# One decode layer on one core: K and V in eight 4 MB transfers instead of sixteen of 2 MB, and the weights in fewer, wider pieces

## The chip, the cores and the metric

The kernel runs on one core of a Trainium2 chip. The metric is the device time of one execution in microseconds (us). A core has five engines that run side by side: TensorE (PE; its weight loads are shown as PEld), VectorE (DVE), ScalarE (ACT), GpSimd (POOL) and SyncE (SP). Sixteen DMA engines move data between the chip's memory and the core's SBUF. SP and ACT issue the transfers, each on a queue of its own (q1 for SP and q10 for ACT in the profile), and each transfer is spread over the DMA engines.

## What is computed

Two sequences (B = 2) with one new token each go through a layer whose attention and MLP both read the same normalised input and are summed. Only the last 2048 of 8192 cached positions count.

```python
xn = layernorm(x)                                   # [2, 1, 576]
q = (xn @ wq).reshape(2, 1, 32, 128)                # 32 query heads, 16 K/V heads, each used by 2
scores = q @ k_cache[:, :, 6144:8192].T * 128**-0.5
o = softmax(scores) @ v_cache[:, :, 6144:8192]
h = relu(xn @ w1 + b1) ** 2                         # 4608 wide
return x + o.reshape(2, 1, 4096) @ wo + (h @ w2 + b2)
```

Everything is bfloat16. K and V are 16.8 MB each after the cut, wq and wo 4.7 MB each, w1 and w2 5.3 MB each: 53.6 MB are read once for an output of 2.3 KB.

## The kernel before

**Units.** A unit `u` is one sequence and four of the 16 K/V heads (`TH = 4`, line 44), so there are eight units (`NU`, line 49). The K of a unit is one 2 MB transfer into a tile of 128 partitions with 16 KB each, and so is its V (`issue_kv`, line 121). Each partition gets 64 consecutive cached rows of one head, which lie together in memory. The pool `kvpool` (line 95) has six such tiles. A tile is refilled only when the tile that stood in it has been read: SP waits for that before it issues the next transfer, and whatever stands behind it on SP waits too.

**One unit's work** is `step(u)` (line 501). TensorE transposes K in eight groups of four 128x128 float32 blocks (`transposes`, line 313; a float32 holds two bfloat16), and ACT and DVE take turns to copy a group from PSUM to SBUF (lines 325 and 327). Three PSUM buffers (`kT`) hold the groups. `scores` (line 329) multiplies the transposed K by the queries, which are laid out with zeros so that one product of 32 columns serves several heads; `softmax` (line 344) takes the maximum (DVE line 346, POOL line 350), the exponential (ACT line 357) and transposes the result (DVE line 360). `pv` (line 364) multiplies V of the unit two before, and `pv_end` (line 376) picks the right head out of each product.

**Weights.** wq and w1 come as 512 full rows, four to a partition, and a remainder of 64 rows cut into two halves of columns (`issue_w`, line 129). wo comes in two halves (`issue_wo`, line 154). w2 comes in four blocks, the last one in three pieces (`issue_w2`, line 162, `W2P`, line 493), so that little work is left after the last piece. What doesn't fit into these blocks, 256 rows, is loaded by ACT in small transfers (`issue_w2x`, line 179): four of five partitions with 9216 bytes, and one of 96 partitions with 1152 bytes. `out_acc` (line 266) adds up all products with wo and w2 in PSUM, four matmuls of 144 columns for each row.

**Order.** TensorE's order is the program's (`keep_in_program_order`, line 105). The transfers of SP are issued in this order: K0, wq in two parts, K1, V0, K2, V1, K3, V2, K4, V3, K5, V4, K6, V5, K7, wo's first half, w1 in two parts, V6, V7, wo's second half, and six pieces of w2. Eight semaphores are handed out in turn to the transfers of both queues, so a transfer also waits until the one eight places before it has landed. After the last piece of w2 come four matmuls, a copy (line 573) and the store of the result (line 574).

Of the kernel before, what the change touches and what calls it, by code (L numbers as in the profile page):

```python
# [16 lines left out]
def kernel(  # L17
# [26 lines left out]
    TH = 4  # L44
# [3 lines left out]
    NQ = Hkv // TH  # L48
    NU = NQ * B
    JG = 8  # L50
    NG = NJ // JG
    UE = NJ * Dh
    NT = 2
    NS = 2 * NT
    NJJ = NJ // NS
    SR = NS * NC
    assert SR == 32 and NG % NT == 0

    NFULL = D // P
    REM = D - NFULL * P  # L60
    S = P // REM
    KC = NFULL + 1
    NXN = NFULL + S
    LQ = (Hq * Dh) // S
    L1 = F // S
    NG4 = 4
    QW = Hq * Dh // NG4
    QB = QW // 2
    QH = QW // Dh
    HW = F // NG4  # L70
    HB = HW // 3
    FR = HW // P
    XS = ((8, 20, 5), (1, 96, 96))
    FT = (HW - sum(r * p for r, p, _ in XS)) // P
    F3 = (NG4 - 1) * HW
    CX = [(r, FT, P) for r in range(FT)]
    FX = []
    for xr, xp, _ in XS:
        FX.append(F3 + FT * P + sum(m * n for m, n, _ in XS[:len(FX)]))
        CX += [(FX[-1] - F3 + r, xr, xp) for r in range(xr)]  # L80
    assert FX[-1] + XS[-1][0] * XS[-1][1] == F
    N3 = (NG4 - 1) * FR
    NFC = N3 + len(CX)
    RB = 32 * (NG4 - 1) + B
# [4 lines left out]
    NP = NQ // 2  # L89
    WR = 2 * NC * Dh // P  # L90
    assert Dh // WR == NC
# [3 lines left out]
    kvpool = ctx.enter_context(tc.tile_pool(name="kvpool", bufs=6))  # L95
    ktpool = ctx.enter_context(tc.tile_pool(name="ktpool", bufs=2))
    wbig = ctx.enter_context(tc.tile_pool(name="wbig", bufs=1))
    wrem = ctx.enter_context(tc.tile_pool(name="wrem", bufs=1))
    wopool = ctx.enter_context(tc.tile_pool(name="wopool", bufs=1))
# [9 lines left out]

    x2d = A_x.rearrange("b s d -> (b s) d")  # L110
    out2d = out.rearrange("b s d -> (b s) d")

    k_tiles, v_tiles, wq_tiles, w1_tiles, wo_tiles, w2_tiles = {}, {}, {}, {}, {}, {}
    WBW = max(Hq * Dh, F)
    WRW = max(LQ, L1)

    def unit_view(cache, u):
        tq, b = divmod(u, B)
        return cache[b, tq * TH:(tq + 1) * TH, S0:Sk, :].rearrange("h (c j) d -> c h (j d)", c=CP)

    def issue_kv(tiles, cache, u, name, parts=1):
        tl = kvpool.tile([P, UE], BF16, tag="kv", name=f"{name}_{u}")
        v = unit_view(cache, u)
        n = UE // parts
        tiles[u] = tl
        return [lambda i=i: nc.sync.dma_start(out=tl[:, i * n:(i + 1) * n], in_=v[:, :, i * n:(i + 1) * n])
# [478 lines left out]
```

## Time and profile before

| what | us |
|---|---|
| median of 3 runs (range) | 134.43 (134.38 to 134.54) |
| the profiled execution | 134.47 |
| its span, first to last instruction | 132.6 |
| PE busy / DVE busy / ACT busy | 84.1 / 57.2 / 46.7 |
| first packet of K0 moves, from the span's start | 2.18 |
| last piece of w2 has landed | 129.43 |
| output's copy ends | 130.08 |

The profiled execution took 134.47 us, 1.9 us more than its span: that much lies outside the first and last instruction. The store and the end of the program take from 130.08 to 132.6. A row of the profile that is cut into slices gives tenths: 9 is a busy share of 90% or more. The DMA row is a mean over the sixteen DMA engines. A chain of waits is followed back from the last instruction: each piece is the time in which the work named was what the next piece waited for.

### The profile page before, as it was taken

To read this page: it belongs to the slowest core of one execution; us is meant where nothing else is said; L and a number is where in the kernel's file an instruction comes from. 1 tells how busy PE (TensorE), PEld (TensorE's weight loads), DVE (VectorE), ACT (ScalarE), POOL (GpSimd) and SP (SyncE) were. 2 spreads that over 40 slices of the span, in tenths; PEclk is the share of its full clock that TensorE was granted. 3 is DMA by queue.
4 is the path that set the end of the run, shared out by engine and by line. 5 is a ranking of instruction groups with operands and counts; after the bars stand their busy time and mean duration, and the time that the engine had idled before them with its cause. 6 is when DMAs were issued, how large, how long until landed. Compare 5 with 4: busy or idle time off the path is not lost.

```text
span 132.6 us, 2337 instructions
## 1 busy us (share of the span) xinstructions
PE 84.1 (63%) x982; PEld 52.2 (39%) x982; DVE 57.2 (43%) x156; ACT 46.7 (35%) x64; POOL 5.2 (4%) x17
## 2 busy tenths in 40 slices
PE   0069409599597669298496599697500938655941
PEld 0068303257364436164254346354300424414930
DVE  6724400525477456566377446575400043344000
ACT  5715500418874375176265255194200040000000
POOL 6000000010010010100100100100100000000000
PEclk9999955958999999999999769999985595555595
DMA  4999999999999999999999999999999999999960
GB/s 139 409 415 488 425 397 416 430 430 415 444 418 431 433 420 427 431 430 430 418 440 420 440 430 432 421 457 432 478 405 388 425 425 450 407 423 428 416 247 1
DMA packets 4219, 53.76 MB, mean 405 GB/s; under 512 B 503, under 2 KB 730, under 8 KB 1246
## 3 DMA queue, kind: packets, MB, share of 16 engines
q1 hardware_dynamic: 4032, 53.32, 94.6%
q10 hardware_dynamic: 178, 0.31, 0.6%
q8 instruction: 7, 0.11, 0.3%
q14 instruction: 2, 0.02, 0.0%
HBM read 53.62 MB, written 0.00 MB: 404 GB/s over the span
## 4 chain that ended last, share of the span: by engine, by line
DMA 62%; PE 4%; DVE 1%; ACT 1%; issue 1%; ACTq 0%
DMA v<-in_A_v_cache_dram 29%; DMA w<-in_B_w_dram 17%; DMA k<-in_A_k_cache_dram 16%; PE kT_ps L108 3%; PE o_ps L105 1%; ACT kT L325 1%; PE sc_ps L105 1%; ACT p L357 1%; DVE pT L360 1%; DVE kT L327 0%; DVE o L386 0%; PE out_ps L105 0%; ACT fin_sb L573 0%; DVE o L384 0%; PE op_ps L105 0%
## 5 line engine op out<-in xcount | busy, mean ns | idle before, releaser
L108 PE MATMUL kT_ps<-ident_f,k 128*128 128x128 f32 x256 | 40.0, 303 | 9.3 <-DMA k<-in_A_k_cache_dram 7.0
L108 PEld LDWEIGHTS kT_ps<-ident_f,k 128*128 128x128 f32 x256 | 31.5, 155 | 22.6 <-issue 11.6
L325 ACT COPY kT<-kT_ps 128x1024 bf16<-128x1024 bf16 x32 | 32.0, 1012 | 21.8 <-PE kT_ps L108 17.4
L327 DVE COPY kT<-kT_ps 128x1024 bf16<-128x1024 bf16 x32 | 21.8, 682 | 12.9 <-PE kT_ps L108 12.7
L105 PE MATMUL sc_ps<-kT,qz 128*32 128x512 bf16 x128 | 10.3, 403 | 6.4 <-DVE kT L327 5.0
L357 ACT ACTIVATE p<-sc_ps,bias 128x512 bf16<-128x512 f32 x8 | 5.5, 688 | 17.6 <-DVE gown L353 17.6
L105 PE MATMUL o_ps<-v,pT 128*32 128x512 bf16 x128 | 11.6, 461 | 0.0
L105 PEld LDWEIGHTS <-xnT 128*2 128x2 bf16 x100 | 3.1, 112 | 17.7 <-issue 17.5
L105 PE MATMUL h_ps<-w_big,xnT 128*2 128x384 bf16 x48 | 3.6, 484 | 7.9 <-DMA w_big<-in_B_w_dram 7.9
L346 DVE TENSOR_REDUCE m<-sc_ps 128x1 f32<-128x512 f32 x8 | 5.5, 692 | 7.1 <-PE sc_ps L105 7.1
L386 DVE SCALAR_TENSOR_TENSOR o<-o_ps,in_s,o 128x128 f32<-128x128 f32 x24 | 8.3, 348 | 0.5
L360 DVE STREAM_TRANSPOSE pT<-p 128x512 bf16<-128x512 bf16 x8 | 5.7, 711 | 6.5 <-ACT p L357 6.5
L573 ACT CAST fin_sb<-out_ps 113x144 bf16<-113x144 f32 x1 | 0.3, 279 | 21.8 <-PE out_ps L105 21.8
L105 PE MATMUL q_ps<-wq_big,xnT 128*2 128x512 bf16 x32 | 3.6, 625 | 5.0 <-DMA wq_big<-in_A_wq_dram 5.0
L350 POOL PARTITION_ALL_REDUCE gmax<-m x8 | 2.9, 365 | 88.8 <-DVE m L348 88.8
L384 DVE TENSOR_SCALAR o<-o_ps,in_s 128x128 f32<-128x128 f32 x8 | 2.7, 341 | 8.1 <-PE o_ps L105 8.1
L451 DVE TENSOR_TENSOR hrow<-t 98x384 bf16<-98x384 f32 x3 | 1.6, 557 | 10.6 <-ACT t L450 10.5
L105 PEld LDWEIGHTS <-qz 128*32 128x32 bf16 x128 | 2.2, 96 | 10.1 <-DVE kT L327 7.5
L105 PE MATMUL op_ps<-o,of_h 128*128 128x129 f32 x16 | 3.9, 333 | 3.2 <-DVE o L386 3.2
L105 PEld LDWEIGHTS <-hT_sb 128*17 128x17 bf16 (+2 forms) x172 | 4.3, 116 | 3.2 <-issue 3.2
L105 PE MATMUL out_ps<-w,hT_sb 128*17 128x144 bf16 x136 | 4.1, 279 | 2.1 <-DMA w<-in_B_w_dram 2.0
L450 ACT ACTIVATE t<-h_ps 98x384 f32<-98x384 f32 x3 | 1.4, 489 | 11.0 <-PE h_ps L105 10.7
(74 smaller groups left out, 52.8 us busy)
## 6 DMA issues: line engine op xcount, KB each, us to landing
k<-in_A_k_cache_dram SPq DMA_DIRECT2D x8, 2048.0 KB, 18.3
v<-in_A_v_cache_dram SPq DMA_DIRECT2D x8, 2048.0 KB, 9.9
wo<-in_A_wo_dram SPq DMA_DIRECT2D x2, 2304.0 KB, 27.2
w_big<-in_B_w_dram SPq DMA_DIRECT2D x1, 4608.0 KB
wq_big<-in_A_wq_dram SPq DMA_DIRECT2D x1, 4096.0 KB, 17.8
w<-in_B_w_dram SPq DMA_DIRECT2D x3, 1296.0 KB, 31.6
w_rem<-in_B_w_dram SPq DMA_DIRECT2D x1, 576.0 KB, 28.0
w<-in_B_w_dram SPq DMA_DIRECT2D x1, 576.0 KB, 22.1
```

Of the source, the lines that this page charges most:

```text
L105: tc.keep_in_program_order(nc.tensor.matmul(*a, **k))
L108: tc.keep_in_program_order(nc.tensor.transpose(*a, **k))
L325: nc.scalar.copy(out=kT, in_=kT_ps[:])
L327: nc.vector.tensor_copy(out=kT, in_=kT_ps[:])
L346: nc.vector.tensor_reduce(out=m1[:], in_=sc_ps[:], axis=AX.X, op=ALU.max)
L350: nc.gpsimd.partition_all_reduce(gmax[:], m2[:], channels=P, reduce_op=ReduceOp.max)
L357: nc.scalar.activation(out=p_sb[:], in_=sc_ps[:], func=ACT.Exp, bias=bias[:, 0:1], scale=scale, accum_out=o1[:, Dh:Dh + 1])
L360: nc.vector.transpose(out=pT[:].rearrange("p j r -> p (j r)"), in_=p_sb[:])
L384: nc.vector.tensor_scalar(scalar1=in_s[:, 0:1], scalar2=None, op0=ALU.mult, **kw)
L386: nc.vector.scalar_tensor_tensor(scalar=in_s[:, k:k + 1], in1=o1[:, 0:Dh], op0=ALU.mult, op1=ALU.add, **kw)
L450: nc.scalar.activation(out=t1, in_=mlp["ps"][k][0:RB, :], func=ACT.Relu)
L451: nc.vector.tensor_tensor(out=hrow[:, k * HB:(k + 1) * HB], in0=t1, in1=t1, op=ALU.mult)
```

## The change

The units become twice as large and half as many: eight K/V heads of one sequence (`TH = 8`), 128 consecutive rows or 32 KB in each partition, four units. A K or V is one 4 MB transfer, `kvpool` holds three of them, and there are sixteen groups of transposes in a step. The scores of a unit are now four banks wide and are computed in four chunks, each followed by its own maximum on DVE; the exponential and the transpose of the result are one instruction each over 2048 columns instead of 512 (and four of each instead of eight). There is one score buffer instead of two. `pv(u)` follows a step of a later unit as a whole: 64 matmuls of 256 columns instead of 16 of 512 for a unit half as large.

wq and w1 are read flat: 4.5 rows in each partition, one transfer each, and the normalised input is laid out with zeros so that each half row meets its own input. wo is one transfer into the same tile that held wq and w1. w2 is two halves of 18 rows in each partition: the first is one transfer, the second has four pieces of 9, 5, 2 and 1 rows, and the last row of each partition comes on ACT's queue in three parts (85, 32 and 11 partitions).

SP has 16 transfers instead of 28, in this order: K0, wq, K1, V0, K2, V1, w1, K3, V2, V3, wo, w2's first half, and four pieces of its second half. The small transfers on ACT's queue are all issued before the first copy of transposed K; before, they were spread over the first 55 us. TensorE's order follows that of the transfers. The waits of SP that come from tiles: K2 for the transposes of K0, V1 for those of K1, K3 for `pv(0)`, V2 for the transposes of K2, V3 for `pv(1)`, wo for the products with w1, w2's halves for the transposes of K3 and for `pv(2)`.

```diff
-    TH = 4
+    TH = 8
...
-    NT = 2
-    NS = 2 * NT
+    NS = 2
...
+    W2P = [(0, 9), (9, 14), (14, 16), (16, 17)]
+    XS = [(0, 85), (85, 117), (117, 128)]
...
-    kvpool = ctx.enter_context(tc.tile_pool(name="kvpool", bufs=6))
-    ktpool = ctx.enter_context(tc.tile_pool(name="ktpool", bufs=2))
+    kvpool = ctx.enter_context(tc.tile_pool(name="kvpool", bufs=3))
     wbig = ctx.enter_context(tc.tile_pool(name="wbig", bufs=1))
-    wrem = ctx.enter_context(tc.tile_pool(name="wrem", bufs=1))
-    wopool = ctx.enter_context(tc.tile_pool(name="wopool", bufs=1))
+    ktpool = ctx.enter_context(tc.tile_pool(name="ktpool", bufs=4))
...
+    def issue_flat(w, name):
+        n = w.shape[0] * w.shape[1] // P
+        tl = wbig.tile([P, NH * L1], BF16, tag="wbig", name=name)
+        nc.sync.dma_start(out=tl[:, 0:n], in_=w.rearrange("r n -> (r n)").rearrange("(p l) -> p l", p=P))
+        return tl
...
+    k_tiles[0] = issue_kv(A_k_cache, 0, "k")
+    wq_sb = issue_flat(A_wq, "wq")
+    k_tiles[1] = issue_kv(A_k_cache, 1, "k")
+    v_tiles[0] = issue_kv(A_v_cache, 0, "v")
...
+    def scores(u, n):
...
+        matmul(sc, lhsT=far_h[:], rhs=is_h, start=True, stop=False, skip_group_check=True)
+        kT = kT_tiles.pop((u, n))[:].rearrange("p (j k c) -> p j k c", k=P, c=2)
+        for c in range(2):
+            for g in range(4):
+                matmul(sc[32 * g:32 * (g + 1), :], lhsT=qz[:, t, b, c, :], rhs=kT[:, :, 32 * g:32 * (g + 1), c],
+                       start=False, stop=(c == 1), skip_group_check=True, tile_position=(0, 32 * g))
+        nc.vector.tensor_reduce(out=m_tiles[u][:, n:n + 1], in_=sc, axis=AX.X, op=ALU.max)
...
     def step(u):
-        fin = None
-        w = u - 2
-        with_pv = w >= 0
-        for g in range(NG):
+        for g in range(NB):
             transposes(u, g)
...
+            n, o = divmod(g, CB)
+            if o == 1 and n > 0:
+                scores(u, n - 1)
+        scores(u, NCH - 1)
         softmax(u)
...
+    for p0, p1 in XS:
+        nc.scalar.dma_start(out=w2x_sb[p0:p1, :], in_=w2_rows[1, p0:p1, (FR - 1) * D:FR * D])
+    k_tiles[2] = issue_kv(A_k_cache, 2, "k")
     step(1)
+    fin = pv(0)
+    v_tiles[1] = issue_kv(A_v_cache, 1, "v")
+    w1_sb = issue_flat(B_w1, "w1")
+    fin()
+    k_tiles[3] = issue_kv(A_k_cache, 3, "k")
+    step(2)
+    fin = pv(1)
+    v_tiles[2] = issue_kv(A_v_cache, 2, "v")
+    fin()
+    mlp_h(w1_sb)
+    v_tiles[3] = issue_kv(A_v_cache, 3, "v")
+    wo_sb = issue_flat(A_wo, "wo")
+    w2b_sb = kvpool.tile([P, (FR - 1) * D], BF16, tag="kv", name="w2b")
+    w2a_sb = kvpool.tile([P, FR * D], BF16, tag="kv", name="w2a")
+    step(3)
+    pv(2)()
+    nc.sync.dma_start(out=w2a_sb[:], in_=w2_rows[0])
+    for r0, r1 in W2P:
+        nc.sync.dma_start(out=w2b_sb[:, r0 * D:r1 * D], in_=w2_rows[1, :, r0 * D:r1 * D])
+    pv(3)()
...
+    out_acc(sel_b[:], xb_sb, 0, start=True)
+    for r in range(WR):
+        out_acc(ws[:, r, :], wo_sb, r)
+    out_acc(hT_sb[:, 1, FR - 1, :], w2x_sb, 0)
+    for r in range(FR):
+        out_acc(hT_sb[:, 0, r, :], w2a_sb, r)
+    for r in range(FR - 1):
+        out_acc(hT_sb[:, 1, r, :], w2b_sb, r, stop=(r == FR - 2))
```

## The prediction

> **What bounds the kernel now.** I read the page first: who is busy, and what the DMA engines do over the span.
>
> ```profile
> span 132.6 us, 2337 instructions
> ...
> PE 84.1 (63%) x982; PEld 52.2 (39%) x982; DVE 57.2 (43%) x156; ACT 46.7 (35%) x64; POOL 5.2 (4%) x17
> ...
> DMA  4999999999999999999999999999999999999960
> ...
> q1 hardware_dynamic: 4032, 53.32, 94.6%
> q10 hardware_dynamic: 178, 0.31, 0.6%
> q8 instruction: 7, 0.11, 0.3%
> ```
>
> No compute engine is above 63%; the DMA engines are full from the first slice to the last but one. The chain of waits (start, duration, what) agrees: from 68 us on it is DMA alone, and 0.65 us of work stands between the last landing and the output.
>
> ```profile
> 68.31 39.02 DMA v<-in_A_v_cache_dram
> 107.33 0.02 issue
> 107.34 22.09 DMA w<-in_B_w_dram
> 129.43 0.04 issue
> 129.47 0.31 PE out_ps L105 x4
> 129.78 0.02 issue
> 129.80 0.28 ACT fin_sb L573
> ```
>
> Then the busy time by stretch (the last three columns: granted clock, DMA share, GB/s).
>
> ```profile
> 40.00:60.00 20.00, 14.82 (x143) 9.07 (x141) 12.05 (x29) 9.46 (x13) 0.73 (x2) 1.00 1.01 428
> 60.00:80.00 20.00, 14.72 (x131) 8.73 (x130) 11.71 (x30) 9.54 (x12) 0.73 (x2) 0.91 1.01 431
> ...
> 126.00:127.00 1.00, 0.00 (x0) 0.00 (x0) 0.00 (x0) 0.00 (x0) 0.00 (x0) 0.94 0.99 393
> 127.00:128.00 1.00, 0.74 (x36) 0.59 (x36) 0.00 (x0) 0.00 (x0) 0.00 (x0) 1.00 0.73 280
> 128.00:129.00 1.00, 0.43 (x16) 0.28 (x16) 0.00 (x0) 0.00 (x0) 0.00 (x0) 1.00 0.41 144
> ```
>
> Two things are to be seen. The queue is never empty (a share over 1 means that packets overlap a little). And the sixteen engines don't stop together: after 127 us more and more are done while others work on. So the end is the load of the slowest engine. Time can only be won by less work on that engine; it is lost by any hole in the queue.
>
> **1. Fewer transfers (gain).** The bytes stay. What does a transfer cost beyond its bytes? I take the first of a transfer's sixteen completions, and its distance to the transfer before, where ACT's queue is quiet. w1's remainder (8 packets of 4608 bytes per engine) took 1.39 us, w1's main part (8 of 36,864) 10.86. A line through both has 36.7 ps per byte and 0.037 us per transfer of 8 packets. It fits the others: 2 MB of K or V 4.85 (measured 4.83 to 4.88), a w2 block 3.08 (3.08 and 3.09). SP has 28 transfers before and 16 after: 12 x 0.037 = 0.44 us less on every engine. The other end comes from the packets' own durations, 611 ns for 16 KB and 1213 for 32 KB: 9 ns for each of 96 packets and 12 completions saved, 0.97 us. As the shares over 1 show that packets overlap, I take 0.44.
>
> [...]
>
> **2. w2's odd rows (loss and gain).** 128 rows move from ACT's queue to SP's: 8 x 1152 bytes x 36.7 ps = 0.34 us more on every engine. The 96-row piece (6 packets of 51 ns on every engine, 0.31) becomes a 32-row and an 11-row piece (2 or 3 packets, 0.10 to 0.15): 0.18 less. With part 1: 0.44 - 0.34 + 0.18 = 0.28 us less on an engine that nothing else disturbs.
>
> **3. The slowest engine (gain).** The last transfer's completions lie at 127.16, 127.18, 127.22 and 127.52, and then twelve from 128.55 to 129.43. Twelve engines are thus some 1.4 us behind. Five of them carry the 5-partition pieces of w2: in the window from 3 to 8 us such a piece shows as ten packets on q10, five of data and five that report, so five engines. Four pieces of 347 ns make 1.39. Seven carry an instruction fetch (q8, 16 KB each): the packet takes 0.88 to 1.06 us and the data packet after it some 0.5 longer than its kind, together about 1.43. 5 + 7 = 12, so no engine had both. One of the five also has the four single-row pieces of b1 (93 ns each) and b2: 0.42 more, which fits the very last one, 129.43.
> After the change the five have 17 pieces of 51 ns, 0.87, and at most 0.25 besides. Then the fetches set the end: undisturbed engines end between 126.88 and 127.24 (0.28 earlier), with 1.43 at 128.3 to 128.7. I take 128.6: **0.83 us earlier** than 129.43. A fetch more (TensorE has 1689 listed instructions for 1480) costs nothing on an engine that has neither burden.
>
> **4. Compute (nothing, under DMA).** Transposes and copies keep their number: 64 copies, 1012 ns on ACT and 682 on DVE. The score area doubles (4 units x 2048 columns for 8 x 512): at the rows' 688, 692 and 711 ns per 512 columns, up to 16 x 0.69 = 11 us instead of 5.5 on ACT for the exponential, and twice that again on DVE for maximum and transpose; DVE loses 20 of its 24 operations of line 386 (348 ns). ACT would be at 52, DVE near 62 us of 132. What hides it is the DMA stream, as long as the next transfer is always issued in time. That is the first rival.
>
> **5. The tail (nothing).** wo now lands whole, near 115 us. Its 128 matmuls (64 took 2.10 us) take 4.2, w2's first 18 rows 2.4 (72 in 2.37), before the next pieces land near 121 and 124. The last piece is one row as before, so 0.65 us of work and the store follow. Without this cover a late `pv(3)` would add its excess; V3 lands near 104, ten us before wo.
>
> **Sum:** 134.47 - 0.83 = 133.64 for the profiled execution, which lies 0.04 above the median: **133.6 us**.
>
> **Rivals.**
>
> *A. The queue runs dry before V1 (slower).* Three 4 MB tiles are fewer buffers than six of 2 MB in time. V1 must wait for K1's last transposes. Start (2.18), and first completions: K0 7.89 + 4.83 = 12.7, wq 10.86 later (w1's row of the same width), K1 at 33.2, on engines with a burden about 34.5; V0 and K2 end at 52.5. The queue has work until about 52.2. K1's transposes start at 34.5; the scores of unit 0 end about then too. Rows for a unit half as large:
>
> ```profile
> 28.34 3.48 PE L108 MATMUL kT_ps<-ident_f,k 128*128 128x128 f32 x20
> ...
> 33.48 1.09 PE L108 MATMUL kT_ps<-ident_f,k 128*128 128x128 f32 x8
> ...
> 36.67 1.09 PE L108 MATMUL kT_ps<-ident_f,k 128*128 128x128 f32 x8
> ...
> 43.30 0.60 PE L108 MATMUL kT_ps<-ident_f,k 128*128 128x128 f32 x4
> ```
>
> 32 transposes with all that lies between them took 28.34 to 34.57 and 36.67 to 43.90: 6.2 and 7.2 us. Twice that is 12.5 to 14.5. There is one score buffer now, so the scores of unit 1 wait for the exponential of unit 0 (about 1.8 us, behind a table load of 1.28), and behind that instruction on TensorE wait ten more groups of transposes; followed group by group I get 14.8, the end at 49.3. Issue to first packet took 1.46 (K0: 0.72 to 2.18), so V1 moves from 50.8: 1.4 us to spare. Against it speaks this sum; for it that it has thirty steps. Each us beyond 50.7 costs one, as engines that are fetched upon later have no slack; from 51.5 the gain is gone, and an end of 53 gives 136. All other waits have over 10 us: K2 is released near 24.5 and needed at 42.9, V2 near 69 and needed at 85, wo near 83 and needed at 104.
>
> *B. 32 KB pieces of eight heads read more slowly (slower).* K and V are 64 packets of 1.21 us on each engine, 77.6 us; each per cent more is 0.78 us, and the change is slower from about 1.1% on. 3% would give 136. For it: the heads lie 2 MB apart in memory, and eight instead of four are read in turn. Against it: K and V run at the line of part 1 with that same distance, and wq's 32 KB packets took 1213 ns. The trace doesn't show eight heads; as bounds I take 2 MB at 4.83 and the slowest 2 MB of the trace, 5.11 with ACT's pieces between them: nothing to 5%.
>
> [...]
>
> *C. One engine gets both burdens (no change).* Fetches may fall on one of the five: 127.4 - 0.28 + 1.43 + 1.1 = 129.65, or 134.7. The trace doesn't name the engines; that seven fetches fell on seven engines of eleven speaks against it.
>
> *D. Packets save what their durations say.* 0.53 more: 133.1.
>
> **How the numbers follow.** Forecast 0.60 (133.1 to 134.1), A 0.13, B 0.08, C 0.11, D 0.08. Below 0.27 us (0.2%) a run of this kernel can't be told from no change. Faster: the forecast, D, and a third of A: 0.72. Same: most of C and some of A: 0.12. Slower: the rest, 0.16. The range goes from 132.9 (D with an early fetch group) to 135.0 (C, and A with a hole of some 1.2 us); it leaves out B and the worst of A.
>
> **What would show it.** Right: DMA share 1.00 in every stretch to 126 us, distance of 4 MB transfers 9.65 to 9.70, last landing near 128.6, and the end set by a few engines about 1.4 us behind the others. A: V1's issue after 50.7 and a DMA share below 1 near 53. B: 4 MB transfers more than 9.8 apart. C: one or two completions over 1 us behind all others. The forecast is wrong if undisturbed engines don't end 0.28 earlier, or if TensorE, not a landing, comes last.

## The result, and the profile after

The changed kernel takes **216.76 us** (median of four, 215.35 to 218.31) where the kernel before takes 134.46 beside it: a ratio of 1.612, 95% interval 1.600 to 1.625. The forecast was 133.6, its range 132.9 to 135.0. The profiled execution took 215.35 us, its span is 213.5.

The page of the changed kernel: busy times, the row of the DMA engines in 40 slices and what they moved, and the queues (packets, MB, share).

```profile
span 213.5 us, 2465 instructions
...
PE 93.4 (44%) x1077; PEld 65.6 (31%) x1077; DVE 62.5 (29%) x136; ACT 48.7 (23%) x55; POOL 3.3 (2%) x12
...
DMA  8999999999999999999999999999998999899991
GB/s 197 196 200 207 372 405 311 199 202 210 223 222 197 204 212 215 209 239 196 209 200 295 443 377 196 246 203 223 215 249 196 227 227 227 220 418 399 429 399 64
...
q1 hardware_dynamic: 2304, 53.46, 96.7%
q10 hardware_dynamic: 194, 0.16, 0.4%
q8 instruction: 8, 0.13, 0.3%
```

The engines of the DMA are as full as before, and the same 53.8 MB are moved. But the row below has two values: some 210 GB/s in most slices, 295 to 443 in three groups. Those groups are wq, w1, and wo with w2. So K and V move at half the rate. The windows (busy time of each engine, then granted clock, DMA share, GB/s) say it once more:

```profile
10.00:20.00 10.00, 0.00 (x0) 0.00 (x0) 0.00 (x0) 0.00 (x0) 0.00 (x0) 1.00 1.01 214
40.00:60.00 20.00, 9.82 (x54) 4.78 (x55) 4.08 (x10) 2.33 (x4) 0.39 (x1) 0.52 0.99 207
60.00:80.00 20.00, 14.06 (x148) 9.43 (x146) 10.62 (x18) 11.29 (x12) 0.39 (x1) 0.84 1.00 209
190.00:200.00 10.00, 3.65 (x97) 2.99 (x90) 1.77 (x6) 0.00 (x0) 0.00 (x0) 0.67 0.99 424
```

From 10 to 20 us K0 is on its way, beside it only 0.04 MB of ACT's small transfers, and no compute engine does anything: 214 GB/s at a share of 1.01. Nothing in the program holds it up. **A full share with half the bytes means that the packets themselves are slow**: a 32 KB packet of K or V takes 2448 ns in the mean, against 1213 for wq's in the kernel before (the median). 1024 such packets on 16 engines make 1024 x 1235 / 16 = 79.0 us of the 80.9 us by which the span grew. The end of the chain of waits (start, duration, what) is of the old kind, a landing and then 1.7 us of work. The landing is that of w2's last piece but two, at 209.15 us; the last row landed at 210.22, while TensorE was at these products.

```profile
172.01 37.13 DMA w2b<-in_B_w_dram
209.19 1.39 PE out_ps L94 x31
210.60 0.28 ACT fin_sb L428
```

### The profile page after: what moved, and what is told of

Same layout as the page of the kernel before. It is cut to its first block, busy times and chain, and to the rows that moved or that the text cites. A ratio compares the mean times of both kernels' runs of the same rounds, so it can differ in the third digit from the quotient of the medians.

```text
span 213.5 us, 2465 instructions
## 1 busy us (share of the span) xinstructions
PE 93.4 (44%) x1077; PEld 65.6 (31%) x1077; DVE 62.5 (29%) x136; ACT 48.7 (23%) x55; POOL 3.3 (2%) x12
## 3 DMA queue, kind: packets, MB, share of 16 engines
q1 hardware_dynamic: 2304, 53.46, 96.7%
## 4 chain that ended last, share of the span: by engine, by line
DMA 64%; PE 18%; another core or an unknown queue 10%; ACT 4%; DVE 2%; issue 1%; SPq 0%
DMA k<-in_A_k_cache_dram 26%; DMA v<-in_A_v_cache_dram 20%; DMA w2b<-in_B_w_dram 17%; PE kT_ps L97 8%; PE o_ps L94 3%; PE sc_ps L94 3%; PE h_ps L94 2%; ACT kT L256 2%; DVE hrow L350 1%; ACT p L288 1%; PE h_ps L97 1%; PE out_ps L94 1%; DVE kT L258 0%; ACT L288 0%
## 5 line engine op out<-in xcount | busy, mean ns | idle before, releaser
L97 PEld LDWEIGHTS kT_ps<-ident_f,k 128*128 128x128 f32 x256 | 37.2, 174 | 57.1 <-DMA k<-in_A_k_cache_dram 49.5
L94 PE MATMUL o_ps<-v,pT 128*32 128x256 bf16 x256 | 12.7, 382 | 26.1 <-DMA v<-in_A_v_cache_dram 26.1
L94 PEld LDWEIGHTS <-pT 128*32 128x32 bf16 x256 | 10.0, 132 | 29.0 <-issue 27.2
L272 DVE TENSOR_REDUCE m<-sc_ps 128x1 f32<-128x512 f32 x16 | 11.0, 689 | 10.8 <-PE sc_ps L94 10.8
L288 ACT ACTIVATE p<-sc_ps,bias 128x2048 bf16<-128x2048 f32 x4 | 7.9, 1967 | 8.6 <-DVE gown L284 8.6
L291 DVE STREAM_TRANSPOSE pT<-p 128x2048 bf16<-128x2048 bf16 x4 | 9.2, 2304 | 0.7 <-ACT p L288 0.7
L94 PE MATMUL sc_ps<-ident,far_h 8*128 8x512 bf16 x16 | 7.0, 438 | 5.3 <-DVE m L272 2.4
L94 PE MATMUL h_ps<-w,xnT 128*4 128x288 bf16 x72 | 4.5, 443 | 9.0 <-DMA w<-in_B_w_dram 9.0
L94 PEld LDWEIGHTS <-xnT 128*4 128x4 bf16 x108 | 3.2, 110 | 13.6 <-issue 11.1
L94 PE MATMUL out_ps<-wo,ws 128*17 128x144 bf16 x128 | 3.6, 304 | 5.4 <-DMA wo<-in_A_wo_dram 5.4
L94 PEld LDWEIGHTS <-hT_sb 128*17 128x17 bf16 x144 | 3.9, 121 | 4.8 <-issue 4.7
```

Of the source, the lines that this page charges most:

```text
L94: tc.keep_in_program_order(nc.tensor.matmul(*a, **k))
L97: tc.keep_in_program_order(nc.tensor.transpose(*a, **k))
L272: nc.vector.tensor_reduce(out=m_tiles[u][:, n:n + 1], in_=sc, axis=AX.X, op=ALU.max)
L288: nc.scalar.activation(out=p_sb[:], in_=sc_ps[:], func=ACT.Exp, bias=bias[:, 0:1], scale=scale, accum_out=o1[:, Dh:Dh + 1])
L291: nc.vector.transpose(out=pT[:].rearrange("p j r -> p (j r)"), in_=p_sb[:])
```

## Experiments

### 1. Which property of the transfers is slow

Three theories came first: (1) heads that lie 2 MB apart meet in the memory, (2) pieces of 32 KB are too long, (3) what counts is the cut into eight heads. `m1_patterns` reads alone (no layer is computed, the output is a copy of x), one pattern after the other into four tiles. Each transfer is `[[stride, blocks], [stride, rows], [1, piece]]` on the memory's side and 128 partitions in SBUF.

> Reads alone, no compute and no result (the output is a copy of x): eight ways to read parts of the K cache into 128 partitions, one after the other. 4 MB each in two transfers, or 2 MB each in four; a: eight heads 2 MB apart in 32 KB pieces (as after); b: four heads in 32 KB pieces; c: eight heads in 16 KB pieces; d: as a, but the heads 2 MB + 4 KB apart; e: flat, 32 KB per partition; f: as a, but the heads 512 KB apart; g: four heads in 16 KB pieces (as before); h: as a, but the heads 2 MB + 32 KB apart. Theory 1 (engines that read the same place of two heads 8 MB apart at the same moment get in each other's way; with eight heads per piece number two of sixteen engines start on the same piece number, with four heads none do): a and c slow (some 19.6 us for 4 MB, as the 2527 ns packets of after make), b, e, g fast (9.7), d and h faster than a, f open. Theory 2 (a 32 KB piece with the next one 2 MB away is slow): a, b, d, h slow; c, e, g fast. Theory 3 (more than four heads read in turn are slow, whatever the place): a, c, d, f, h slow; b, e, g fast.

The timeline of DVE in this run; each line is a copy that waits for one transfer, and the idle time in brackets plus the 0.16 us of the copy before it is the time that transfer took (a: 8 heads of 32 KB pieces as after; b: 4 heads of 32 KB; c: 8 heads of 16 KB; d, f, h: eight heads 2 MB + 4 KB, 512 KB, 2 MB + 32 KB apart; e: flat; g: 4 heads of 16 KB as before; c and g are 2 MB, the others 4).

```profile
43.26 0.16 DVE L57 COPY acc<-pa 128x1 bf16<-128x1 bf16 x1 [19.79 <-DMA pa<-in_A_k_cache_dram]
...
63.05 0.16 DVE L57 COPY acc<-pb 128x1 bf16<-128x1 bf16 x1 [9.99 <-DMA pb<-in_A_k_cache_dram]
...
82.53 0.16 DVE L57 COPY acc<-pc 128x1 bf16<-128x1 bf16 x1 [9.65 <-DMA pc<-in_A_k_cache_dram]
...
142.16 0.16 DVE L57 COPY acc<-pd 128x1 bf16<-128x1 bf16 x1 [19.81 <-DMA pd<-in_A_k_cache_dram]
...
161.97 0.16 DVE L57 COPY acc<-pe 128x1 bf16<-128x1 bf16 x1 [10.01 <-DMA pe<-in_A_k_cache_dram]
...
201.81 0.16 DVE L57 COPY acc<-pf 128x1 bf16<-128x1 bf16 x1 [19.82 <-DMA pf<-in_A_k_cache_dram]
...
211.50 0.16 DVE L57 COPY acc<-pg 128x1 bf16<-128x1 bf16 x1 [4.74 <-DMA pg<-in_A_k_cache_dram]
...
261.53 0.16 DVE L57 COPY acc<-ph 128x1 bf16<-128x1 bf16 x1 [19.76 <-DMA ph<-in_A_k_cache_dram]
```

Whatever has 16 blocks of 8 (a, c, d, f, h) takes 19.4 to 20.0 us per 4 MB. Whatever has 32 blocks of 4 or is flat takes half of that: b and e 9.6 to 10.2, g 4.8 to 5.4 per 2 MB. Neither the distance of the heads nor the length of a piece matters. The kernel says the same in the next two runs.

```diff
 e_halves:  each K and V as two transfers of half the columns, pieces of 16 KB
-        nc.sync.dma_start(out=tl[:], in_=...)
+        for i in range(2):
+            nc.sync.dma_start(out=tl[:, z], in_=v[:, :, z])     # z: half i of the columns
 e_stagger: heads 2 MB - 32 KB apart; the last positions of heads 1 to 7 are left out
+        in_=bass.AP(cache.tensor, o, [[UE, CP], [(Sk - 128) * Dh, TH], [1, UE]])
```

> After, with each 4 MB transfer of K and V issued as two of 2 MB: the first and the second 16 KB of every partition. The heads and the partitions stay. Theory 1 (two engines meet at the same place of two heads): 16 KB packets near 1.23 us instead of 0.61, some 215 us. Theory 2 (long pieces far apart): packets of 0.61, some 134 us. Theory 3 (eight heads): some 215 us.

> After, with the heads read 2 MB minus 32 KB apart: head h of a transfer starts 128*h cached positions earlier, so the last positions of heads 1 to 7 are left out and as many before the window are read in their place. Packets stay 32 KB and eight heads are read in turn; engines that started on the same place of two heads are now 128 KB apart. Theory 1: packets of 1.21 us, and the time that was forecast for the change, 133 to 135 us. Theories 2 and 3: some 215 us.

`e_halves` took 212.3 us (one execution), its 16 KB packets 1201 ns in the mean instead of 616: theory 2 falls. `e_stagger` took 217.3 (ratio to before 1.620, 1.617 to 1.623): theory 1 falls. `m2_shapes` (reads alone, output a copy of x) took the memory out: rows 32 KB + 256 bytes apart, nearly one stretch, cut into blocks in different ways.

```python
qa = [[132224, 16], [16512, 8], [1, 16384]]     # and qb 32 x 4, qc 64 x 2, qd 8 x 16, 128 partitions
qe = [[16512, 64], [1, 16384]]                  # 64 partitions, 0 to 63; qf the same into 32 to 95
qg = [[66176, 16], [16512, 4], [1, 16384]]      # 0 to 63; qh into 32 to 95
```

> Reads alone, no compute and no result (the output is a copy of x). 32 KB pieces whose addresses are nearly one flat block (32 KB + 256 bytes apart), so that no place in memory is special. 4 MB into 128 partitions, two transfers each, as 16 blocks of 8 pieces (a), 32 of 4 (b), 64 of 2 (c), 8 of 16 (d). Then 2 MB into 64 partitions, two each: in one row into partitions 0 to 63 (e) and 32 to 95 (f), and as 16 blocks of 4 into 0 to 63 (g) and 32 to 95 (h). Theory P (the outermost dimension sets which partitions an engine writes; with blocks of 8 partitions the sixteen engines write at any moment into half of the lanes to SBUF): a 19.6 us for 4 MB, b and c 9.7, d 19 or more; e and g, all in the lower half of the partitions, 9.7 for 2 MB; h 4.9, f 4.9 or between. Theory Q (the places in memory): a as fast as b, 9.7. Theory R (a shape of 16 blocks costs the engines time wherever it lands): a slow; g and h both slow, e and f equal.

The timeline of DVE (four copies of 0.17 us behind each transfer):

```profile
43.56 0.68 DVE L57 COPY acc<-qa 32x1 bf16<-32x1 bf16 x4 [19.30 <-DMA qa<-in_A_k_cache_dram]
...
62.88 0.68 DVE L57 COPY acc<-qb 32x1 bf16<-32x1 bf16 x4 [9.04 <-DMA qb<-in_A_k_cache_dram]
72.59 0.68 DVE L57 COPY acc<-qc 32x1 bf16<-32x1 bf16 x4 [9.03 <-DMA qc<-in_A_k_cache_dram]
...
185.33 0.68 DVE L57 COPY acc<-qd 32x1 bf16<-32x1 bf16 x4 [42.97 <-DMA qd<-in_A_k_cache_dram]
```

16 blocks of 8 still took 20.0 us per 4 MB, 32 of 4 and 64 of 2 took 9.6 to 9.7 (the last one, beside the next pattern, 10.6), 8 of 16 took 44 and 58 with eight completions instead of sixteen. So it isn't the memory but **how the cut deals the partitions to the engines**. The 64-partition part of this run told nothing (4.8 to 13.4 us per 2 MB): "8 of 16" ahead of it had only eight completions, so the engines can't have begun it together.

`e_four` puts 32 blocks of 4 into the changed kernel. K and V are then read from four heads and 4096 positions, so they are not the reference's.

```diff
-        in_=cache[b, t * TH:(t + 1) * TH, S0:Sk, :].rearrange("h (c j) d -> c h (j d)", c=CP)
+        in_=cache[b, t * TH:t * TH + 4, Sk - 2 * W:Sk, :].rearrange("h (c j) d -> c h (j d)", c=2 * CP)
```

> After, with each 4 MB transfer of K and V read from four heads, 4096 positions each, instead of eight heads with 2048: a source of 32 blocks of 4 pieces of 32 KB into the same 128 partitions. Instructions, packets, buffers and waits stay; K and V hold other data than the reference's, so this is for the time alone. If only the read rate of K and V was wrong in the prediction: 4 MB in 9.7 us and 133.0 to 134.1 us in all. If other steps failed too (the queue dry before V1, engines with two burdens, the tail): above 134.5, with the DMA share below 1 near 53 us or one or two completions far behind the others.

136.37 us (ratio 1.018, 1.011 to 1.025); packets of K and V at a median of 1213 ns. The window in which `after` moved 209 GB/s:

```profile
60.00:80.00 20.00, 15.05 (x192) 10.22 (x196) 12.44 (x24) 8.05 (x8) 0.39 (x1) 0.91 0.99 425
```

The cut is worth 80 of the 82 us. The other 2 are treated in section 3.

### 2. Why the cut is slow

I took it that with 16 blocks each of the sixteen engines gets one block, eight partitions in a row; 8 blocks gave eight completions, which fits. Theory 3a is that the places in SBUF decide: engines that write certain places at the same moment get in each other's way. Its "half of the ways" is an estimate from the halved rate (20.0 us per 4 MB for 9.6). That it puts 0 to 63 on the slow side and 32 to 95 on the fast one, and which engines disturb each other, was my assumption. Theory 3b is that the cut itself costs time. How 32 blocks of 4 and 64 of 2 are dealt out isn't shown; the runs show only that they are fast (9.6 to 9.7 us). `m3_places` and `m4_offset` (reads alone, output a copy of x) were to tell the two apart, and with blocks 128 elements further apart `m3b_places` and `m4b_offset`.

```python
ra = [[16512, 64], [1, 16384]]                     # m3, m3b: into 0 to 63; rb into 32 to 95
rc = [[66048, 16], [16512, 4], [1, 16384]]         # m3: into 0 to 63; rd into 32 to 95 (m3b: 66176)
# m4: blocks x rows, first partition; [[rows * 16512, blocks], [16512, rows], [1, 8192]]  (m4b: + 128)
t_1 16x8 0; t_2 16x8 0; d_4 4x4 0; t_3 16x8 0; t_4 16x8 0; d_12 12x4 32; t_5 ... t_8 16x8 0
# m5: t_1 t_2 d_8 (8x4 32) t_3 ... t_6;  m6: t_1 t_2 d_12 t_3 t_4 d_4 t_5 ... t_8, both spaced as m4b
```

> Reads alone (twelve transfers of 2 MB, 32 KB to each of 64 partitions, rows 32 KB + 256 bytes apart in memory; the layer isn't computed, the output is a copy of x). Three flat ones into partitions 0 to 63, three flat ones into partitions 32 to 95, then three of 16 blocks of 4 partitions into 0 to 63, and three of 16 blocks of 4 into 32 to 95. So far every transfer cut into 16 blocks of 8 partitions took 19.4 to 19.9 us per 4 MB, every one cut into 32 blocks of 4, 64 of 2 or flat 9.6 to 9.9. Theory 3a, the places in SBUF decide: with 16 blocks each engine has one block, eight partitions in a row, and all sixteen engines write at the same moment into only half of the ways into SBUF. [...] By 3a a transfer into 0 to 63 takes about 9.7 us per 2 MB in either cut, and one into 32 to 95 about 4.9 in either cut. Theory 3b, the cut itself costs time (an outermost dimension of 16 on the memory's side): flat ones 4.9 wherever they land, the 16 blocks of 4 9.7 wherever they land. If all four are 4.9, it is neither: then only blocks of eight are slow. All 9.7: 64 partitions are simply half of the engines' room, and nothing is told apart.

> Reads alone (the layer isn't computed, the output is a copy of x), all issued at once into tiles of their own, nothing waits. Eight transfers t1 to t8 of 2 MB in the slow cut, 16 blocks of 8 partitions, 16 KB each. Between t2 and t3 stands a read of 4 blocks of 4 rows of 16 KB, between t4 and t5 one of 12 blocks of 4 rows. A transfer cut into 8 blocks had only eight completions, so I expect the first of these reads on 4 engines and the second on 12, each engine busy for four pieces, 2.4 us: the length of half a block of eight. Theory 3a (places in SBUF): engines that stand half a block apart write into different ways and no longer disturb each other. [...] t1 and t2 9.65 us each on all. After the first read 0 to 3 stand half a block behind 4 to 7: these eight take 4.85 us for each of t3 and t4, the other eight 9.65: completions of t4 near 31 us (four), 34 (four) and 41 (eight). After the second 8 to 11 stand behind 12 to 15 as well, and all take 4.85: completions of t8 in four groups of four, near 53, 55, 60 and 63 us, the last packet near 63. Theory 3b (the cut costs time) or anything in memory: every transfer takes 9.65 on every engine whatever stands before it: t8 ends near 80 to 84 us, in groups only 2.4 us apart.

Both missed their condition: the blocks stood exactly one block apart, so the compiler joined the dimensions and nothing was cut. `m3_places` gave 10.1 and 4.9 us per 2 MB for the two places, `m4_offset` 4.6 to 6.0 for every transfer. With the blocks further apart:

> As m3_places (reads alone, output a copy of x): flat transfers of 2 MB into partitions 0 to 63 (three) and 32 to 95 (three), then 16 blocks of 4 partitions into 0 to 63 and 32 to 95. In m3_places the blocks stood exactly 4 rows apart, so the compiler had joined both dimensions into one of 64 rows (its instructions show 64x16384 for all twelve), and the second half only repeated the first: 10.1 us into 0 to 63, 4.9 into 32 to 95. Now the blocks stand 256 bytes further apart and can't be joined. [...] Theory 3b (an outermost dimension of 16 costs time itself): 10 or more in both.

The timeline of DVE again (ra: flat into partitions 0 to 63, rb: flat into 32 to 95, rc and rd: 16 blocks of 4 into the same places; 2 MB each):

```profile
23.85 0.32 DVE L57 COPY acc<-ra 32x1 bf16<-32x1 bf16 x2 [9.87 <-DMA ra<-in_A_k_cache_dram]
...
43.73 0.32 DVE L57 COPY acc<-rb 32x1 bf16<-32x1 bf16 x2 [4.53 <-DMA rb<-in_A_k_cache_dram]
...
69.30 0.32 DVE L57 COPY acc<-rc 32x1 bf16<-32x1 bf16 x2 [9.97 <-DMA rc<-in_A_k_cache_dram]
...
88.93 0.32 DVE L57 COPY acc<-rd 32x1 bf16<-32x1 bf16 x2 [4.53 <-DMA rd<-in_A_k_cache_dram]
```

The place decides (10.2 and 10.3 us into 0 to 63, 4.9 into 32 to 95), and 16 blocks cost nothing in the right one: 3b falls. Why these places differ isn't shown. Now the engines were to be set apart in time:

> As m4_offset (reads alone, output a copy of x), whose blocks had been joined by the compiler into flat rows too (128x8192, 4.9 us per 2 MB from the first transfer on), so that it didn't hold the slow cut at all. Now the blocks stand 256 bytes further apart than eight rows. Expected is what stood there. Theory 3a: t1 and t2 9.65 us each on all engines. After the read of 4 blocks, engines 0 to 3 stand half a block behind 4 to 7: these eight take 4.85 us for each of t3 and t4, the other eight 9.65: completions of t4 near 31 us (four), 34 (four) and 41 (eight). After the read of 12 blocks all are offset, and each transfer takes 4.85: completions of t8 in four groups of four near 53, 55, 60 and 63 us. Theory 3b, or anything in memory: 9.65 for every transfer on every engine; t8 ends near 80 to 84.

```profile
23.27 0.68 DVE L75 COPY acc<-t 32x1 bf16<-32x1 bf16 x4 [9.00 <-DMA t<-in_A_k_cache_dram]
27.78 0.14 DVE L75 COPY acc<-d 16x1 bf16<-16x1 bf16 x1 [3.82 <-DMA d<-in_A_k_cache_dram]
37.55 0.68 DVE L75 COPY acc<-t 32x1 bf16<-32x1 bf16 x4 [9.62 <-DMA t<-in_A_k_cache_dram]
46.99 0.69 DVE L75 COPY acc<-t 32x1 bf16<-32x1 bf16 x4 [8.76 <-DMA t<-in_A_k_cache_dram]
51.38 0.32 DVE L75 COPY acc<-d 32x1 bf16<-32x1 bf16 x2 [3.71 <-DMA d<-in_A_k_cache_dram]
56.81 0.68 DVE L75 COPY acc<-t 32x1 bf16<-32x1 bf16 x4 [5.11 <-DMA t<-in_A_k_cache_dram]
62.17 0.68 DVE L75 COPY acc<-t 32x1 bf16<-32x1 bf16 x4 [4.68 <-DMA t<-in_A_k_cache_dram]
```

From line to line, the same transfers took 9.4 to 9.8 us until the second added read (d) and 5.4 or less after it. The time doesn't belong to the transfer; it goes with what was read ahead of it. Half of the expectation failed: behind the first added read, of 4 blocks, which was to put four engines half a block behind, all stayed slow. So 3a became the theory 3a': engines e and e + 4 of each eight are pairs, and one pair that meets holds up all sixteen.

> Reads alone as in m4b_offset (output a copy of x): t1 and t2, then a read of 8 blocks of 4 pieces (on eight engines), then t3 to t6, all 2 MB in 16 blocks of 8. m4b showed: with four engines half a block behind nothing changes (9.6 us per transfer on all); with four more steps, when four stand at 0, eight at a half and four at a whole block, all run at 5.3 us. Theory 3a': engines 0 and 4, 1 and 5, 2 and 6, 3 and 7, 8 and 12 to 11 and 15 are pairs whose partitions lie in the same ways, and one pair that meets holds up all sixteen. Here 0 to 7 move together, so every pair still meets: 9.6 us per transfer, t6 ends near 60. Rival 3a'': no pairs, only the numbers count; the ways of the first and of the second half of each block are two pools, and eight engines on each are enough: t3 to t6 take 4.9 to 5.3 us each, the end comes near 45.

> m4b_offset with both reads exchanged (reads alone, output a copy of x): 12 blocks of 4 pieces between t2 and t3, 4 blocks between t4 and t5. Theory 3a' (pairs, one that meets holds up all): after the first the pairs 0/4 to 3/7 still meet, so t3 and t4 take 9.6 us on all engines; after the second 0 to 3 stand a whole block behind 12 to 15 and half a block behind 4 to 7, every pair is apart, and t5 to t8 take 5.3 us each: as in m4b the end comes near 72. Rival: what came in m4b after the second read came from the read of 12 alone or from the moment: then t3 is fast here already (end near 58), or t5 to t8 stay slow (end near 85).

`m5_eight` after its added read (the timeline goes on like that):

```profile
37.17 0.68 DVE L74 COPY acc<-t 32x1 bf16<-32x1 bf16 x4 [9.42 <-DMA t<-in_A_k_cache_dram]
46.88 0.69 DVE L74 COPY acc<-t 32x1 bf16<-32x1 bf16 x4 [9.03 <-DMA t<-in_A_k_cache_dram]
```

9.5 to 9.7 us for every transfer, though 8 blocks were to put eight engines on each half: two pools fall. `m6_reversed`, both reads exchanged, after the first (d, 27.78) and the second (51.75):

```profile
27.78 0.33 DVE L77 COPY acc<-d 32x1 bf16<-32x1 bf16 x2 [4.04 <-DMA d<-in_A_k_cache_dram]
37.33 0.68 DVE L77 COPY acc<-t 32x1 bf16<-32x1 bf16 x4 [9.22 <-DMA t<-in_A_k_cache_dram]
47.01 0.68 DVE L77 COPY acc<-t 32x1 bf16<-32x1 bf16 x4 [9.00 <-DMA t<-in_A_k_cache_dram]
51.75 0.14 DVE L77 COPY acc<-d 16x1 bf16<-16x1 bf16 x1 [4.06 <-DMA d<-in_A_k_cache_dram]
56.81 0.68 DVE L77 COPY acc<-t 32x1 bf16<-32x1 bf16 x4 [4.91 <-DMA t<-in_A_k_cache_dram]
```

Both as 3a' has it. In the kernel itself (all computed, 2 MB more read):

```diff
 e_offset:  ahead of K0; e_offset2: behind K0, into K1's tile, and ACT's transfers merged (b1 one, w2 one)
+    for n, p0 in ((12, 32), (4, 0)):
+        nc.sync.dma_start(out=tile[p0:p0 + 4 * n, :], in_=A_k_cache[0, 0:n, 0:512, :].rearrange(
+            "h (r j) d -> h r (j d)", r=4))
```

> The kernel after, computing all of it, with two reads more at the head of SP's queue, 12 blocks and 4 blocks of four 32 KB pieces (2 MB that nobody uses). By theory 3a' they set the engines half a block of K apart. K0, K1, V0 and K2 then run near full rate, 9.7 to 10.7 us each on an engine instead of 19.9; the engines in front run dry before V1, which waits for K1's transposes (by about 60 us), all start V1 together, and from there on every 4 MB takes 19.9 again: V1 82, w1 93, K3 113, V2 133, V3 153, wo 164, w2 176, execution near 181 us instead of 216, though it reads 2 MB more. Where the weights' flat transfers meet K's the engines may be held up for some us: up to 195. Rival (the cut is slow as such): 216 plus 4.9 to 9.7 us, 221 to 226.

230.9 us (ratio 1.713): K0 was issued late (at 9.38 us) and by 3a' only four engines stood apart from the others, so this run tells nothing of the full offset.

> e_offset said nothing about the offset: K0 had to wait until the first of the added reads had landed (the eight semaphores of the transfers are handed out in turn), so it was issued at 9.38 us and twelve engines began it together; only 0 to 3 stood apart, which by m4b frees nobody. Now the two added reads (12 blocks and 4 blocks of four 32 KB pieces, into the tile that K1 overwrites) stand behind K0 and ahead of wq, and ACT's transfers are fewer (b1 in one, w2's last rows in one), so that none of SP's first transfers waits for a semaphore. All of the layer is computed. Theory 3a' (pairs of engines that meet hold up all): K0 takes 20 us as before; after the reads the engines stand at 0, a half and a whole block, and K1, V0 and K2 take 9.7 to 12 us each on an engine. K1 lands near 54 as in the kernel after (2 MB more were read before it), V1 is issued near 70 as there (72.95), but by then V0 and K2 are through, where after still had 20 us of K2 to go. The engines run dry, start V1 together and are slow again: span 185 to 195 instead of 213.5. Rival (the cut is slow as such, or the memory): the added reads only add, 218 to 228.

213.5 us (211.3 to 217.6), with 2 MB more than the kernel after at 216.8. The profiled span is 211.0 us instead of 185 to 195, so of 18 to 28 us forecast 2.5 are there. The completions show why. wq, which stands ahead of K1, took 14 us on eight engines and 19 on the last four instead of 10.9: by 3a' a new meeting, since four were in K1 while it was read flat. K1 so landed at 65.3 us instead of 56.1. Then V0 and K2 took 11.0 to 12.9 us on an engine (one 13.7) instead of 19.9, and K2 had landed at 90.3 us instead of 96.7. V1 was issued only at 86.46, where 70 was expected, and the engines ran dry:

```profile
80.00:90.00 10.00, 8.88 (x119) 5.21 (x117) 5.67 (x12) 4.04 (x5) 0.39 (x1) 0.89 0.64 218
```

So the added reads speed up the cut in the kernel too, but most of the gain was lost to a cost that I had put at "some us" and to the wait for V1.

### 3. The other two microseconds

`e_four` landed last at 130.84 us, where the steps of the prediction gave 128.6. V1 was issued at 52.63 instead of 49.3, and the windows of `e_four` (last columns: DMA share, GB/s) show the hole:

```profile
52.00:53.00 1.00, 0.92 (x7) 0.46 (x5) 0.68 (x2) 0.80 (x1) 0.00 (x0) 1.00 0.76 328
53.00:54.00 1.00, 0.61 (x16) 0.38 (x20) 0.33 (x1) 0.22 (x1) 0.00 (x0) 1.00 0.75 246
54.00:55.00 1.00, 1.00 (x47) 0.98 (x40) 0.87 (x3) 0.00 (x0) 0.00 (x0) 1.00 1.35 426
55.00:56.00 1.00, 0.75 (x28) 0.46 (x20) 0.49 (x4) 0.00 (x0) 0.39 (x1) 1.00 0.54 229
```

```diff
 e_four_w1:   the line  w1_sb = issue_flat(B_w1, "w1")  moved from behind V1 to behind K2
 e_four_both: the same, and
-    XS = [(0, 85), (85, 117), (117, 128)]
+    XS = [(0, 128)]
```

> e_four (K and V in 32 blocks of 4 partitions, other positions of other heads than the reference's) with w1 issued right after K2, ahead of V1, which must wait for the transposes of K1; w1 needs only the tile of wq, free since about 31 us. e_four took 135.97 us in its profiled execution (median 136.37) where step 1 to 5 of the prediction gave 133.6. Theory H: most of the remaining difference is the hole before V1 (rival A). By the bytes of the windows from 51 to 57 us of e_four (1949 units of 1 GB/s x 1 us instead of 2592) the hole cost 1.5 us, of which 0.3 came back after it. If so, the DMA share stays near 1 from 50 to 58 us, and the execution takes 134.6 to 135.0. Rival: the hole costs nothing because engines that are behind for other reasons (instruction fetches, ACT's pieces) catch up in it: 135.7 to 136.1, with the last completions spread further apart.

> As e_four_w1, and w2's last row of each partition in one piece of 128 partitions instead of three of 85, 32 and 11. In e_four eleven completions of the last transfer lay by 129.56 and five from 130.48 to 130.84; a piece of 85 partitions falls on five engines, 17 packets of 51 ns each. In one piece every engine has 8. Step 3 of the prediction (the engines with the pieces of ACT's queue and those with instruction fetches set the end): the five lose up to 12 packets, 0.6 us, the eleven others gain 5 to 6, 0.3 us: the end comes 0.6 us earlier than in e_four_w1, at 134.0 to 134.4. Rival: the five are behind for another reason, and nothing changes.

The last landing moved by about what was expected: 129.63 with the hole filled (-1.2), 129.17 with w2's last rows in one piece as well (-0.46). But the second step isn't shown to be the even piece's work: the first completion of the last transfer moved by the same 0.46 (127.67 to 127.21), and K0's had already come 0.55 earlier (13.52 to 12.97).

The time didn't follow: 135.91 us (134.2 to 136.4, ratio 1.007, 1.004 to 1.010) and 135.11 (134.0 to 136.0, ratio 1.003, 0.9995 to 1.007). Most executions lie in two groups about 1.5 us apart, the lower ones (134.2 to 134.9, and 134.0 to 134.2) near or within what was expected. What makes the groups isn't shown. The profiled executions are both of the upper group. The end of the chain of `e_four_both`:

```profile
118.91 3.63 PE o_ps L94 x33
125.27 3.05 PE out_ps L94 x183
128.32 0.97 issue
129.29 1.62 PE out_ps L94 x89
```

TensorE is late here; from 24.8 us on the chain holds no landing at all. For 0.97 us TensorE stood still amid the products with w2's first half, which had landed by 123.25, and waited for nothing that the profile shows. Before that, `pv(3)` had started at 118.91 us, in `e_four` at 111.27, though V3 landed earlier (106.27 for 107.90). One reason can be read. The product `op_ps`, which ends a `pv`, waits for DVE's line 311, and with w1 moved DVE does its transpose of line 291 (2.31 us) ahead of that line at `pv(1)` and `pv(2)`; in `e_four` it does so behind it. `op_ps` of `pv(1)` in `e_four`, then in `e_four_both`:

```profile
76.79 0.46 PE L94 MATMUL op_ps<-o,of_h 128*128 128x129 f32 x2 [1.03 <-DVE o L311]
```

```profile
85.96 0.77 PE L94 MATMUL op_ps<-o,of_h 128*128 128x129 f32 x2 [5.52 <-DVE o L311]
```

So 1.62 us of products stand behind the last landing instead of the 0.31 of the kernel before. What the DMA won, TensorE took.

`b_even` tested step 3 on the kernel before: ACT's small transfers dealt evenly.

```diff
 b_even: w2's four pieces of 5 partitions (every fourth of 20) -> partitions 0 to 15 and 16 to 19; b1 4 rows in one
 b_b1:   b1 alone
-    for i in range(0, NG4, NG4 // 4):
-        nc.scalar.dma_start(out=b1_sb[i:i + NG4 // 4, :], in_=b1_rows[i:i + NG4 // 4, :])
+    for i in range(0, NG4, NG4):
+        nc.scalar.dma_start(out=b1_sb[i:i + NG4, :], in_=b1_rows[i:i + NG4, :])
```

> The kernel before, with the small transfers of ACT's queue dealt evenly: w2's four pieces of 5 partitions become one of 16 and one of 4, and the four single rows of b1 one transfer. Step 3 of the prediction said that five engines end late because of those pieces (four of 347 ns each, and on one of them four rows of 93 ns), and seven because of instruction fetches, all of them 1.4 us behind the four others. If that holds, the five end about 0.7 us earlier (one piece of 347 ns more than now on no engine but four), the seven 0.35 later, and the last landing comes from 129.43 to 128.9 or 129.3: 133.9 to 134.3 us instead of 134.4. Rival: what is behind at the end is not these engines, and the time stays within 0.2% of before.

> The kernel before with one of b_even's two edits: the four rows of b1 in one transfer (four partitions). b_even took 136.8 us where 134.1 was expected. In its trace 4 to 10 us from the start brought 1754 instead of 2489 GB/s x us, 1.7 us of the stream, at the time of the piece of 16 partitions. [...] Then b1's edit alone costs nothing: 134.3 to 134.6. [...]

`b_even` took 136.84 us (ratio 1.017, 1.016 to 1.019), `b_b1` 134.77 (1.003, 1.0015 to 1.0047). The window from 4 to 10 us of before, of `b_even` and of `b_b1`:

```profile
4.00:10.00 6.00, 2.19 (x14) 2.08 (x15) 2.69 (x14) 2.41 (x5) 0.00 (x0) 1.00 0.99 415
```

```profile
4.00:10.00 6.00, 0.52 (x6) 0.40 (x6) 2.70 (x14) 1.88 (x4) 0.00 (x0) 1.00 1.00 292
```

```profile
4.00:10.00 6.00, 2.06 (x13) 1.95 (x14) 2.69 (x14) 2.27 (x5) 0.00 (x0) 1.00 0.98 412
```

The same share, 123 GB/s less: (415 - 292) x 6 / 431 = 1.7 of the 2.4 us, for 0.15 MB from ACT. The piece put sixteen engines on partitions 0 to 15 (in 2 to 12 us q10 has 40 packets, for 20 partitions' data and as many that report), and its packets of 9216 bytes took up to 999 ns instead of 347. That fits what was found for K and V, but no run put the sixteen partitions elsewhere, so here it is argued and not shown. `b_even` says nothing on step 3. b1 alone costs 0.3%, just above what was expected.

## Why the prediction was wrong, step by step

- **What bounds the kernel, and the line of step 1** (36.7 ps per byte and 0.037 us per transfer). Here it failed: I let a transfer's time follow from its bytes and packets alone. All rows that made the line were flat or cut into 32 blocks of 4. The profile before has no row of 16 blocks of 8, and I didn't bound that as an unknown cost of step 1. The 64 packets of K and V on each engine, put at 1.21 us, took 2.45, and the first completions of neighbouring 4 MB transfers lie 18.7 to 19.9 us apart instead of 9.65 to 9.70.
- **Rival B** named the right transfers and the wrong reason. Its "against it" was true and beside the point: 2 MB distance and 32 KB packets are harmless (`m1_patterns` b and e), and other distances don't help (d, f, h). Its upper bound, 5% from a 2 MB transfer beside ACT's pieces, was taken from the fast kind of cut; the measured price was 102%. Four heads 2 MB apart ran at full rate (b 9.6 and 10.2 us per 4 MB, g 4.8 to 5.4 per 2 MB), eight at half of it whatever the pitch (a, d, f, h: 19.8 to 20.1 per 4 MB).
- **Step 1's gain and step 2** held once the cut was mended, except at the start. In `e_four_both` 4 MB transfers lie 9.66 to 9.71 us apart, and from K0's first completion to that of the last piece 114.24 us pass, where the forecast had 126.88 - 12.72 = 114.16. But K0's first completion came at 12.97 (13.27 and 13.52 in `e_four` and `e_four_w1`) instead of 12.7. The last landing is 129.17 against 129.43 before and 128.6 forecast: a third of the gain of 0.83 is there.
- **Step 3** (instruction fetches set the end, the pieces of w2 stay within 0.87 + 0.25) is borne out. In `e_four` ten completions of the last piece lie at 128.92 to 129.56 and six at 130.48 to 130.84 (before `e_four_both` I had counted eleven and five and suspected ACT's 85 partitions). ACT's pieces had all landed by 42.8 us, and behind the hole 15 engines end V1 within 0.8 us. From there the late ones come one by one, a fetch each (begun at 53.2, 66.2, 80.7, 97.2, 112.6 and 122.9 us): one engine is late at V1, two at w1, three at K3 and V2, four at V3, five at wo, six at the end. `e_four_both` ends alike, after six fetches: nine at 127.21 to 127.71, one at 128.13, six at 128.74 to 129.17. Both groups are some 0.4 us later than forecast (126.88 to 127.24 and 128.3 to 128.7).
- **Step 4 with rival A**: it happened. K1's transposes ended by 52.63 instead of 49.3, and the hole cost 1.2 us. The sum had 1.4 us to spare and 3.3 us of error. K0 landed at 13.3 to 13.6 instead of 12.7, the scores of unit 0 ended at 37.3 instead of "about 34.5", each chunk behind a 0.70 us maximum on DVE. In `e_four_w1` and `e_four_both`, with the hole filled, compute isn't under the DMA any more: behind wq the chain runs through it alone.
- **Step 5** held in `e_four` (0.67 us of work behind the last landing at 130.84) and failed as soon as w1 was put ahead of V1.

The account of the kernel after, in packet time per engine: 79.0 us from K and V; 3.2 from the weights, whose means are above the undisturbed packet, 1485 ns for 1364 (wq and wo, 256 packets) and 1689 for 1533 (w1, 128), probably where they met engines still in K or V; 1.2 less because 1024 packets of 1213 ns take the place of 2048 of 616. That makes 81.0, and the span grew by 80.9; smaller terms are left out. The hole of rival A comes to light only with the cut mended.

No version beat the kernel before. `e_four_both` comes within 0.3% with other data; with the reference's eight heads I know no cut into 32 blocks or more that keeps the layout of 128 rows of one head per partition.

## What to carry to other kernels

Read a DMA-bound profile as two rows, the share of the engines and the GB/s: a full share at half the bytes is not a lack of transfers but slow packets (here a share of 1.01 at 214 GB/s, and 2448 ns for 1213). Before a transfer gets a new access pattern, look at its outermost dimension on the memory's side, which in these runs decided how fast 128 partitions were filled; a pattern that the trace has not shown is an unknown cost, however well the bytes are known. Here 128 partitions ran at full rate flat and in 32 or 64 blocks (9.6 to 10.6 us per 4 MB), and at half of it or less in 16 (20.0) or 8 (44 and 58). Distrust small transfers into few neighbouring partitions (`b_even`: packets of up to 999 ns for 347). And where a few engines end late, follow them back from transfer to transfer: when each fell behind says more than how many there are.

## What the runs showed of the hardware

- Transfers into 128 partitions in 16 blocks of 8 ran at 207 to 214 GB/s (`after`), the other cuts at 424 to 431 (`before`, `e_four`, the weights in `after`). Read alone they took about 20 us per 4 MB instead of 9.6 to 10.6, for every distance in memory tried (33 KB to 2 MB + 32 KB) and for pieces of 16 and 32 KB (`m1_patterns`, `m2_shapes`).
- 64 partitions took about 10.1 us per 2 MB as 0 to 63 and 4.9 as 32 to 95, flat or in 16 blocks of 4 (`m3_places`, `m3b_places`).
- Transfers in 16 blocks of 8 took 9.4 to 9.8 us per 2 MB behind one added read of 4, 8 or 12 blocks, and 4.7 to 5.4 behind reads of 4 and of 12 (`m4b_offset`, `m5_eight`, `m6_reversed`). That one pair of engines that meets holds up the others is the plainest reading I have. No run shows which engines meet, or how the others are held.
- A cut into 4, 8 and 12 blocks gave 4, 8 and 12 completions. That these are engines 0 to k - 1 and that engine e has block e was assumed; m5 and m6 came out as that assumption has it.
- In `e_four` six of the last piece's sixteen completions came about 1 us behind the other ten (130.48 to 130.84 us for 128.92 to 129.56), behind six instruction fetches (a 16 KB packet of 0.88 to 1.07 us each), one more late behind each.
- 256 bytes between blocks decided whether the compiler joined two dimensions, and so how fast the transfers ran: `m4_offset` and `m4b_offset` differ by nothing else, and by 23 us (53.8 and 77.0).
